# Mixture-of-experts and Fourier mixing in one kernel: tokens and residuals side by side in the first half of a step, comparisons between the halves, GELU rounded by ACT

## The chip, the cores and the metric

The kernel runs on one core of a Trainium2 chip. The time is device microseconds of one execution; the median of three runs stands for a kernel. Engines are named as in the profile: PE (matmuls), DVE (vector), ACT (activations), POOL (indirect DMAs here), SP (the queue of plain DMAs). Each works through its instructions in order.

## The reference, cut to what matters

```python
# x: 2048 tokens x 448; 8 experts, hidden width 1792, top 2
g = sigmoid((x * gate_w).sum(-1))
a = Re(DFT_seq(DFT_hidden(x)))              # given as four dense matrices
gates = softmax(x @ wg); cw = the two largest gates of a token, normalised, else 0
h = gelu(einsum("nd,edf->nef", x, w1))      # tanh form
b = einsum("ne,ned->nd", cw, einsum("nef,efd->ned", h, w2))
out = g * a + (1 - g) * b
```

All inputs and the output are fp32.

## The kernel before

The Fourier part runs first, folded by the symmetries of the given matrices. Whether the matrices have these symmetries is compared on the device, beside the experts' work: `quad_check` compares tiles of them (`quads`) on DVE, and a general path at the end runs only where a comparison fails. Then each token goes to two experts. A routing generator (`routing`, lines 239 to 443) sorts tokens into experts in small pieces on DVE, with two short matmul groups on PE (lines 373 and 404); `advance` runs its next pieces, two in each step of expert 0.

The experts are 112 jobs of 14 steps each, (e, f): expert e, the 128 hidden columns f. The experts are sorted by load, and `CAPS` is the number of tokens that each takes: 576, 544, 544, 544, 512, 512, 512, 496. Every fp32 operand is kept as two parts, a rounded one and the residual that the rounding leaves, so that a product is three matmul passes at the fast rate for rounded operands. The names are:

- `hi`, `lo`: the first weight matrix of a step, rounded by ACT (`upper`, line 205) and its residual by DVE (`lower`, line 210); `up`, `dn`: the same for the second matrix. Both are made two steps ahead (`prep`).
- `XH`, `XL`: the expert's tokens, transposed, in four chunks of 128 rows (`NC`); XL holds three, because the fourth chunk carries 64 token rows and their residuals together. They are filled for the next expert by `gather` (POOL), `blocks` (DVE transposes into `xq`) and `turn` (ACT rounds, DVE subtracts).
- `acc`: three PSUM banks for the up product; `g`: GELU of it (ACT, line 748), two buffers; `gh`, `gl`: `g` rounded (DVE, line 756) and the residual (DVE, line 757), three buffers each; `y`: the sums of the down product, one bank for 128 tokens.

`up(u)` does the up product of job u. With more than 512 tokens it takes two halves (`nh = 2`), each 11 matmuls into one bank: `hi` with XH and with XL for three chunks, `hi` with the fourth chunk of XH, `lo` with the four chunks of XH. `down(u)` does three matmuls of 448 columns for each 128 tokens. With 32 tokens over (experts 1 to 3, `apart`) these are set aside in `rest` and come at the end of an expert (`few`); expert 0 has 64 over and takes them as a fifth tile.

The main loop writes iteration u in this order: `turn`, `prep(u + 2)`, routing pieces (expert 0), `stage` (DVE transposes and gathers), `up(u + 1)`, `down(u)`, `side_work(u)`. PE, DVE, ACT and SP keep the order in which the code is written (`manual_schedule`), and waits are semaphores between the queues. `side_work(u)` issues the DMAs of `quads`, does one quarter of a unit of comparisons (from step 15 on; a unit of four steps has 1, 2, 2 and 3 comparisons of 512 columns, and in later units four of 256 columns against `near`, all in its first step), the blends of the Fourier part (in the fourth and sixth step of experts 1 to 4), and later mixes and sends.

Of the kernel before, what the change touches and what calls it, by code (L numbers as in the profile page):

```python
# [10 lines left out]
F32R = mybir.dt.float32r  # L11
# [3 lines left out]
AF = mybir.ActivationFunctionType  # L15
OP = mybir.AluOpType
AX = mybir.AxisListType

P = 128
# [4 lines left out]
NC = 4  # L24
E = 8
F = 1792
NF = F // P
CAPS = (576, 544, 544, 544, 512, 512, 512, 496)
CMAX = max(CAPS)
# [10 lines left out]
Q = 32  # L40
# [22 lines left out]
def r32(ap):  # L63
    return ap.bitcast(F32)
# [7 lines left out]
def tile_kernel(ctx: ExitStack, tc: tile.TileContext, xt, xrows, xplain, wg, whid, cq, cw, cspec, edge, refs, wquad, whall, cgen, wcat, out):  # L72
# [450 lines left out]
    XH, XL = {}, {}  # L523
# [125 lines left out]
    def turn(e, c):  # L649
        if c == 0:  # L650
            XH[e] = xp.tile([P, NC, CMAX], F32R, name="XH")
            XL[e] = xp.tile([P, NC - 1, CMAX], F32R, name="XL")
        k, xq = XQ.pop((e, c))
        src = xq[:, :k].rearrange("p q c t -> p c q t")
        sl = slice(c * P, c * P + k * Q)
        h = XH[e][:, :, sl].rearrange("p c (q t) -> p c q t", t=Q)
        l = XL[e][:, :, sl].rearrange("p c (q t) -> p c q t", t=Q)
        se.activation(h, src, AF.Copy)
        ve.tensor_tensor(l, src[:, : NC - 1], r32(h[:, : NC - 1]), OP.subtract)
        ve.tensor_tensor(h[64:P, NC - 1], src[64:P, NC - 1], r32(h[64:P, NC - 1]), OP.subtract)  # L660

    def turn0(c, n):
        if c == 0:
            XH[0] = xp.tile([P, NC, CMAX], F32R, name="XH")
            XL[0] = xp.tile([P, NC - 1, CMAX], F32R, name="XL")
        pt = (psy if c > 1 else ps).tile([P, NC, P], F32, name=f"y{c - 2}" if c > 1 else "acc")
        xg = XG.pop(c)
        for k in range(NC):
            te.transpose(pt[:, k, :n], xg[:n, k * P : (k + 1) * P], ident[:n, :n])
        sl = slice(c * P, c * P + n)  # L670
        se.activation(XH[0][:, :, sl], pt[:, :, :n], AF.Copy)
        TU[c] = pt, sl, n
# [3 lines left out]
    def left0(c):  # L676
        pt, sl, n = TU.pop(c)
        ve.tensor_tensor(XL[0][:, :, sl], pt[:, : NC - 1, :n], r32(XH[0][:, : NC - 1, sl]), OP.subtract)  # L678
        ve.tensor_tensor(XH[0][64:P, NC - 1, sl], pt[64:P, NC - 1, :n], r32(XH[0][64:P, NC - 1, sl]), OP.subtract)
# [51 lines left out]
    def up(u):  # L731
# [6 lines left out]
        cut = 2 * P if u == 0 else cap // nh  # L738
        for hf in range(nh):
            cs = slice(hf * cut, cap if hf == nh - 1 else cut)  # L740
            n = cs.stop - cs.start
            acc = ps.tile([P, 512], F32, name="acc")
            part = lambda w, x, c: (w[:, c * P : (c + 1) * P], x[e][:, c, cs])
            steps = [part(hi, XH, c) for c in range(NC - 1)] + [part(hi, XL, c) for c in range(NC - 1)]
            steps += [part(hi, XH, NC - 1)] + [part(lo, XH, c) for c in range(NC)]
            for s, (a, b) in enumerate(steps):
                te.matmul(acc[:, :n], a, b, start=s == 0, stop=s == len(steps) - 1)  # L747
            se.activation(g[:, cs], acc[:, :n], AF.Gelu_apprx_tanh)  # L748
# [7 lines left out]
        ve.tensor_copy(gh[:, :top], g[:, :top])  # L756
# [117 lines left out]
    def quad_check(q, s):  # L874
# [3 lines left out]
        if part < 2:  # L878
# [10 lines left out]
            if s:  # L889
                return  # L890
            if col < 8 * NQT:
                rt["near"] = ck.tile([P, 2, 256], F32, name="near", bufs=1)
                se.activation(rt["near"].rearrange("p c n -> p (c n)"), row(0)[:, :512], AF.Copy)
                return
            for k in range(4):
# [116 lines left out]
    def side_work(s):  # L1012
# [12 lines left out]
        if 1 <= e <= NQT and f in (3, 5):  # L1025
            blend(2 * (e - 1) + f // 5)
# [16 lines left out]
    for u in range(UP, last):  # L1043
# [15 lines left out]
        up(u + 1)  # L1059
        if u < last - 3:  # L1060
            down(u)
        side_work(u - UP)
# [205 lines left out]
```

## Time and profile before

| | us |
|---|---|
| median of 3 runs | 637.38 |
| the runs | 636.42, 637.38, 637.40 |
| the profiled execution | 636.95 |
| its span, first to last instruction | 635.0 |

| engine | busy us (share of the span) | instructions |
|---|---|---|
| PE | 625.5 (99%) | 3721 |
| DVE | 506.1 (80%) | 1258 |
| ACT | 248.1 (39%) | 504 |
| POOL | 204.8 (32%) | 194 |

The span's start and end are those of the program on the core; 1.95 us of the execution lie around it. A matmul's listed duration covers its way through the array and overlaps the next one's, so what a matmul costs is read from the starts of two that follow each other. Of DVE and ACT instructions the listed ends overlap the next start by some hundredths to a tenth of a microsecond too. "[0.57 <-ACT g]" at the end of a timeline row says that the engine idled 0.57 us before it and what ended that.

### The profile page before, as it was taken

To read this page: it belongs to the slowest core of one execution; us is meant where nothing else is said; L and a number is where in the kernel's file an instruction comes from. 1 tells how busy PE (TensorE), PEld (TensorE's weight loads), DVE (VectorE), ACT (ScalarE), POOL (GpSimd) and SP (SyncE) were. 2 spreads that over 40 slices of the span, in tenths; PEclk is the share of its full clock that TensorE was granted. 3 is DMA by queue.
4 is the path that set the end of the run, shared out by engine and by line. 5 is a ranking of instruction groups with operands and counts; after the bars stand their busy time and mean duration, and the time that the engine had idled before them with its cause. 6 is when DMAs were issued, how large, how long until landed. Compare 5 with 4: busy or idle time off the path is not lost. (4 is left out here: it accounts for less than half of the span.)

```text
span 635.0 us, 11162 instructions
## 1 busy us (share of the span) xinstructions
PE 625.5 (99%) x3721; PEld 564.1 (89%) x3721; DVE 506.1 (80%) x1258; ACT 248.1 (39%) x504; POOL 204.8 (32%) x194
## 2 busy tenths in 40 slices
PE   9999999999999999999999999999999999999995
PEld 5999999999998999989999788888888888888884
DVE  7889797589987899779997699987997788556561
ACT  2553233344344444343443434333343434444450
POOL 1210084553153141443340343433331432141123
PEclk9999999999999999999999999999999999999998
DMA  8546454487677766786676957779576736766754
GB/s 345 187 148 211 159 181 140 160 200 260 199 253 194 211 220 218 234 206 207 207 234 203 245 164 237 251 221 291 161 234 195 152 114 151 166 129 151 149 82 67
DMA packets 58752, 122.79 MB, mean 193 GB/s; under 512 B 8288, under 2 KB 31984, under 8 KB 58688
## 3 DMA queue, kind: packets, MB, share of 16 engines
q1 hardware_dynamic: 47376, 101.95, 49.0%
q0 software_dynamic: 11168, 20.00, 17.7%
q8 instruction: 31, 0.51, 0.3%
q14 instruction: 33, 0.27, 0.1%
q10 hardware_dynamic: 144, 0.07, 0.0%
HBM read 105.89 MB, written 16.08 MB: 192 GB/s over the span
## 5 line engine op out<-in xcount | busy, mean ns | idle before, releaser
L748 ACT ACTIVATE g<-acc 128x272 f32<-128x272 f32 (+4 forms) x168 | 77.9, 466 | 311.1 <-issue 179.7
L637 POOL DMA_INDIRECT xg<-xrows,piece x115 | 120.2, 1045 | 223.4 <-DVE xq L646 150.0
L790 PE MATMUL y<-up,gh 128*128 128x448 f32 (+1 forms) x458 | 167.7, 366 | 0.0
L790 PE MATMUL y<-dn,gh 128*128 128x448 f32 (+1 forms) x458 | 167.6, 366 | 0.0
L747 PE MATMUL acc<-XH,hi 128*128 128x272 f32 (+4 forms) x672 | 163.6, 324 | 0.0
L790 PE MATMUL y<-up,gl 128*128 128x448 f32 (+1 forms) x444 | 162.8, 367 | 0.1
L747 PE MATMUL acc<-XH,lo 128*128 128x272 f32 (+4 forms) x672 | 135.0, 323 | 0.0
L747 PEld LDWEIGHTS acc<-XH,hi 128*128 128x128 f32 x672 | 115.6, 188 | 9.3 <-issue 1.1
L747 PEld LDWEIGHTS acc<-XH,lo 128*128 128x128 f32 x672 | 105.8, 188 | 8.7 <-DVE lo L210 0.2
L756 DVE CAST gh<-g 128x512 fp32r<-128x512 f32 (+2 forms) x111 | 47.8, 431 | 81.2 <-ACT g L748 74.9
L747 PE MATMUL acc<-XL,hi 128*128 128x272 f32 (+4 forms) x504 | 107.8, 322 | 0.0
L843 POOL DMA_INDIRECT out<-ys,tok x36 | 62.0, 1723 | 115.6 <-ACT ys L839 69.7
L790 PEld LDWEIGHTS y<-up,gh 128*128 128x128 f32 (+1 forms) x458 | 85.8, 187 | 8.0 <-DVE ys L837 0.2
L790 PEld LDWEIGHTS y<-dn,gh 128*128 128x128 f32 (+1 forms) x458 | 85.8, 187 | 7.8
L790 PEld LDWEIGHTS y<-up,gl 128*128 128x128 f32 (+1 forms) x444 | 83.2, 187 | 7.9 <-DVE gl L757 0.4
L884 DVE CUSTOM_DVE_ANT_0 junk<-quads 128x512 f32<-128x512 f32 x128 | 88.1, 688 | 2.5 <-DMA quads<-cq 0.3
L747 PEld LDWEIGHTS acc<-XL,hi 128*128 128x128 f32 x504 | 81.0, 188 | 6.9 <-DVE XL L678 0.2
L757 DVE TENSOR_TENSOR gl<-g,gh 128x512 fp32r<-128x512 f32 (+1 forms) x111 | 76.7, 691 | 10.5 <-DVE gh L756 0.5
L210 DVE TENSOR_TENSOR lo<-raw,hi 128x512 fp32r<-128x512 f32 x112 | 77.1, 688 | 2.1 <-ACT hi L205 1.0
L205 ACT ACTIVATE hi<-raw 128x512 fp32r<-128x512 f32 x112 | 69.7, 622 | 0.0
L210 DVE TENSOR_TENSOR dn<-row,up 128x448 fp32r<-128x448 f32 x112 | 69.2, 618 | 0.0
L205 ACT ACTIVATE up<-row 128x448 fp32r<-128x448 f32 x112 | 63.5, 567 | 0.0
(263 smaller groups left out, 388.5 us busy)
## 6 DMA issues: line engine op xcount, KB each, us to landing
quads<-cq SPq DMA_DIRECT2D x64, 512.0 KB
raw<-wcat SPq DMA_DIRECT2D x112, 256.0 KB
row<-wcat SPq DMA_DIRECT2D x112, 224.0 KB
out<-yt SPq DMA_DIRECT2D x21, 224.0 KB
xraw<-xt SPq DMA_DIRECT2D x8, 512.0 KB
out<-ot POOLq DMA_DIRECT2D x16, 224.0 KB
cw<-cw SPq DMA_DIRECT2D x4, 512.0 KB
xg<-xrows,piece POOLq DMA_INDIRECT x115
```

Source lines behind the costliest of these rows:

```text
L205: se.activation(hi[:, : raw.shape[-1]], raw, AF.Copy)
L210: ve.tensor_tensor(lo[:, :n], raw, r32(hi[:, :n]), OP.subtract)
L637: st = gp.indirect_dma_start(out=xg[:, q], out_offset=None, in_=xrows, in_offset=bass.IndirectOffsetOnAxis(ap=rt["piece"][:, e, g : g + 1] ...
L747: te.matmul(acc[:, :n], a, b, start=s == 0, stop=s == len(steps) - 1)
L748: se.activation(g[:, cs], acc[:, :n], AF.Gelu_apprx_tanh)
L756: ve.tensor_copy(gh[:, :top], g[:, :top])
L757: ve.tensor_tensor(gl[:, :main], g[:, :main], r32(gh[:, :main]), OP.subtract)
L790: te.matmul(Y[c][:m, :D], a, b, start=f == 0 and s == 0, stop=f == NF - 1 and s == len(steps) - 1)
L843: st = gp.indirect_dma_start(out=out, out_offset=bass.IndirectOffsetOnAxis(ap=rt["tok"][:n, e, c : c + 1], axis=0), in_=ys[:n], in_offset= ...
L884: ve.tensor_tensor_reduce(out=junk[:, :512], in0=row(a[0])[:, a[1] * 512 : a[1] * 512 + 512], in1=row(b[0])[:, b[1] * 512 : b[1] * 512 + 5 ...
```

## The change

It does four things, in experts 0 to 3 (those with more than 512 tokens) except where said.

1. XH and XL become one tile `X` of seven chunks: 0 to 3 the rounded tokens, 4 to 6 the residuals.
2. The first half of a step is 256 columns wide (it was half of the tokens, 288 or 272, apart from step 0). For chunks 0 to 2 one matmul of 512 columns takes the 256 rounded columns and the 256 residual columns of a chunk with the same weights, into the two halves of one bank. The fourth chunk and `lo` go into the bank's first half alone. So the first half has 8 matmuls in place of 11. ACT copies the residual sums to `g`, DVE adds the other half to them, and ACT does GELU in place. The second half (320 or 288 columns) is as before. Step 0 keeps its old first half.
3. `gh` is rounded by ACT instead of DVE. In experts 4 to 7 DVE still does it.
4. `side_work` is called between the two halves of `up(u + 1)` instead of behind `down(u)`; in experts 4 to 7 it stays behind. The near comparisons are spread, three in the first step of a unit and one in the second, for all experts. The blends move to the third and the last step of an expert.

```diff
     def turn(e, c):
         if c == 0:
-            XH[e] = xp.tile([P, NC, CMAX], F32R, name="XH")
-            XL[e] = xp.tile([P, NC - 1, CMAX], F32R, name="XL")
+            X[e] = xp.tile([P, 2 * NC - 1, CMAX], F32R, name="X")
...
-        h = XH[e][:, :, sl].rearrange("p c (q t) -> p c q t", t=Q)
-        l = XL[e][:, :, sl].rearrange("p c (q t) -> p c q t", t=Q)
+        h = X[e][:, :NC, sl].rearrange("p c (q t) -> p c q t", t=Q)
+        l = X[e][:, NC:, sl].rearrange("p c (q t) -> p c q t", t=Q)
...
-    def up(u):
+    def up(u, between=lambda: None):
...
-        cut = 2 * P if u == 0 else cap // nh
+        cut = 2 * P
         for hf in range(nh):
...
-            part = lambda w, x, c: (w[:, c * P : (c + 1) * P], x[e][:, c, cs])
-            steps = [part(hi, XH, c) for c in range(NC - 1)] + [part(hi, XL, c) for c in range(NC - 1)]
-            steps += [part(hi, XH, NC - 1)] + [part(lo, XH, c) for c in range(NC)]
-            for s, (a, b) in enumerate(steps):
-                te.matmul(acc[:, :n], a, b, start=s == 0, stop=s == len(steps) - 1)
-            se.activation(g[:, cs], acc[:, :n], AF.Gelu_apprx_tanh)
+            part = lambda w, x, c: (w[:, c * P : (c + 1) * P], X[e][:, x + c, cs], n)
+            both = nh > 1 and hf == 0 and u > 0
+            if both:
+                steps = [(hi[:, c * P : (c + 1) * P], X[e][:, c : c + NC + 1 : NC, cs], 2 * n) for c in range(NC - 1)]
+            else:
+                steps = [part(hi, 0, c) for c in range(NC - 1)] + [part(hi, NC, c) for c in range(NC - 1)]
+            steps += [part(hi, 0, NC - 1)] + [part(lo, 0, c) for c in range(NC)]
+            for s, (a, b, m) in enumerate(steps):
+                te.matmul(acc[:, :m], a, b, start=s == 0, stop=s == len(steps) - 1)
+            if both:
+                se.activation(g[:, cs], acc[:, n : 2 * n], AF.Copy)
+                ve.tensor_tensor(g[:, cs], acc[:, :n], g[:, cs], OP.add)
+            se.activation(g[:, cs], g[:, cs] if both else acc[:, :n], AF.Gelu_apprx_tanh)
+            if hf == 0:
+                between()
...
-        ve.tensor_copy(gh[:, :top], g[:, :top])
+        if nh > 1:
+            se.activation(gh[:, :top], g[:, :top], AF.Copy)
+        else:
+            ve.tensor_copy(gh[:, :top], g[:, :top])
         ve.tensor_tensor(gl[:, :main], g[:, :main], r32(gh[:, :main]), OP.subtract)
...
-            if s:
-                return
             if col < 8 * NQT:
+                if s:
+                    return
...
-            for k in range(4):
+            for k in ((0, 1, 2), (3,), (), ())[s]:
...
-        if 1 <= e <= NQT and f in (3, 5):
-            blend(2 * (e - 1) + f // 5)
+        if 1 <= e <= NQT and f in (2, NF - 1):
+            blend(2 * (e - 1) + f // (NF - 1))
...
-        up(u + 1)
+        split = CAPS[jobs[u + 1][0]] > 512
+        up(u + 1, lambda: side_work(u - UP) if split else None)
         if u < last - 3:
             down(u)
-        side_work(u - UP)
+        if not split:
+            side_work(u - UP)
```

`turn0` and `left0`, which fill the tokens of expert 0, change only in the names of the tiles.

How the instructions stand is shown at three places. The first is DVE's queue in expert 0, one step with the routing's `oa` compares. Before:

```order
L756 CAST gh<-g 128x576 [waits Activation_49]
L757 TENSOR_TENSOR gl<-g,gh 128x512 [waits DVE_49]
L764 TENSOR_TENSOR gh<-g,gh 128x64
L210 TENSOR_TENSOR lo<-raw,hi 128x512 [waits DMAHW7_49,PE_49,Activation_49]
L210 TENSOR_TENSOR dn<-row,up 128x448 [waits DMAHW0_49,PE_49,Activation_49]
L360 TENSOR_TENSOR oa<-sr,one 128x1024 x2
```

The same step with the change:

```order
L752 TENSOR_TENSOR g<-acc,g 128x256 [waits Activation_49]
L767 TENSOR_TENSOR gl<-g,gh 128x512 [waits Activation_49]
L774 TENSOR_TENSOR gh<-g,gh 128x64
L210 TENSOR_TENSOR lo<-raw,hi 128x512 [waits DMAHW7_49,Activation_49]
L210 TENSOR_TENSOR dn<-row,up 128x448 [waits DMAHW0_49,Activation_49]
L360 TENSOR_TENSOR oa<-sr,one 128x1024 x2
```

The add takes the cast's place, and `gl`, which waited for the cast on its own engine, now waits for ACT. The second place is ACT's queue in the same step. Before:

```order
L748 ACTIVATE g<-acc 128x288 [waits DVE_49,PE_49,Activation_49]
L748 ACTIVATE g<-acc 128x288 [waits PE_49]
L205 ACTIVATE hi<-raw 128x512 [waits DMAHW5_49]
L205 ACTIVATE up<-row 128x448 [waits DMAHW6_49]
L748 ACTIVATE g<-acc 128x288 [waits DVE_49,PE_49,Activation_49]
```

With the change:

```order
L751 ACTIVATE g<-acc 128x256 [waits PE_49]
L753 ACTIVATE g<-g 128x256 [waits DVE_49]
L753 ACTIVATE g<-acc 128x320 [waits PE_49]
L764 ACTIVATE gh<-g 128x576 [waits Activation_49]
L205 ACTIVATE hi<-raw 128x512 [waits DMAHW5_49]
L205 ACTIVATE up<-row 128x448 [waits DMAHW6_49]
```

The first GELU stands behind a wait for DVE's add, and the rounding stands between the second GELU and the next step's weights. The third place is PE's up product in expert 1. Before, one half of it:

```order
L747 MATMUL acc<-XH,hi 128x272 [waits Activation_49]
L747 MATMUL acc<-XH,hi 128x272 x2
L747 MATMUL acc<-XL,hi 128x272 x3
L747 MATMUL acc<-XH,hi 128x272
L747 MATMUL acc<-XH,lo 128x272 [waits DVE_49]
L747 MATMUL acc<-XH,lo 128x272 x3
```

With the change, the first half and the start of the second:

```order
L749 MATMUL acc<-X,hi 128x512 [waits Activation_49]
L749 MATMUL acc<-X,hi 128x512 x2
L749 MATMUL acc<-X,hi 128x256
L749 MATMUL acc<-X,lo 128x256 [waits DVE_49]
L749 MATMUL acc<-X,lo 128x256 x3
L749 MATMUL acc<-X,hi 128x288 [waits DVE_49]
```

Six matmuls have become three, and the second half's bank is now released by DVE (the add that read it last) instead of ACT.

## Rows read from the trace of the kernel before

**Rows 1.** The page: busy time of PE, and the clock that TensorE was granted in 40 slices of the span, in tenths.

```profile
PE 625.5 (99%) x3721; PEld 564.1 (89%) x3721; DVE 506.1 (80%) x1258; ACT 248.1 (39%) x504; POOL 204.8 (32%) x194
...
PEclk9999999999999999999999999999999999999998
```

**Rows 2.** PE's timeline, one step of expert 2 (start us, duration, engine, line, operation and tiles, count): start of the first half, start of the down product, start of the next step.

```profile
206.49 0.54 PE L747 MATMUL acc<-XH,hi 128*128 128x272 f32 x3
...
209.26 0.36 PE L790 MATMUL y<-up,gh 128*128 128x448 f32 x1
...
211.73 0.54 PE L747 MATMUL acc<-XH,hi 128*128 128x272 f32 x3
```

**Rows 3.** PE's timeline, one step of expert 0 and the routing's matmul group behind it.

```profile
64.17 0.56 PE L747 MATMUL acc<-XH,hi 128*128 128x288 f32 x3
...
67.09 0.37 PE L790 MATMUL y<-up,gh 128*128 128x448 f32 x1
...
69.98 0.98 PE L373 MATMUL acc<-vtok,oa 128*128 128x40 f16 x32
```

**Rows 4.** PE's timeline at other widths: from the first `XL` matmul of step 0's first half (256 columns) to its second half, and one step of expert 5 (512 columns) to the next.

```profile
38.15 0.52 PE L747 MATMUL acc<-XL,hi 128*128 128x256 f32 x3
...
39.10 0.60 PE L747 MATMUL acc<-XH,hi 128*128 128x320 f32 x3
...
422.93 0.86 PE L747 MATMUL acc<-XH,hi 128*128 128x512 f32 x3
423.62 0.84 PE L747 MATMUL acc<-XL,hi 128*128 128x512 f32 x3
...
425.43 0.36 PE L790 MATMUL y<-up,gh 128*128 128x448 f32 x1
...
427.87 0.86 PE L747 MATMUL acc<-XH,hi 128*128 128x512 f32 x3
```

**Rows 5.** DVE's timeline in expert 0, from one cast to the next.

```profile
56.62 0.46 DVE L756 CAST gh<-g 128x576 fp32r<-128x576 f32 x1
57.11 0.69 DVE L757 TENSOR_TENSOR gl<-g,gh 128x512 fp32r<-128x512 f32 x1
...
58.99 2.36 DVE L360 TENSOR_TENSOR oa<-sr,one 128x1024 bf16<-128x1024 bf16 x2
61.92 0.46 DVE L756 CAST gh<-g 128x576 fp32r<-128x576 f32 x1 [0.57 <-ACT g L748]
```

**Rows 6.** Groups of instructions with shapes kept apart (busy us, mean ns of one, idle before), ACT and DVE.

```profile
L205 ACT ACTIVATE hi<-raw 128x512 fp32r<-128x512 f32 x112 | 69.7, 622 | 0.0
...
L748 ACT ACTIVATE g<-acc 128x320 f32<-128x320 f32 x1 | 0.4, 437 | 1.4 <-PE acc L747 1.4
...
L748 ACT ACTIVATE g<-acc 128x256 f32<-128x256 f32 x1 | 0.4, 383 | 1.2 <-PE acc L747 1.2
...
L990 DVE TENSOR_TENSOR ot<-fold 128x225 f32<-128x225 f32 x16 | 6.2, 390 | 0.0
...
L678 DVE TENSOR_TENSOR XL<-acc,XH 128x384 fp32r<-128x384 f32 x2 | 1.1, 553 | 0.0
```

**Rows 7.** ACT's timeline in expert 0: a second half's GELU, and two GELUs without a wait between them.

```profile
61.47 0.41 ACT L748 ACTIVATE g<-acc 128x288 f32<-128x288 f32 x1 [1.01 <-PE acc L747]
...
98.88 0.71 ACT L748 ACTIVATE g<-acc 128x288 f32<-128x288 f32 x2 [5.59 <-PE acc L747]
```

**Rows 8.** DVE's timeline in expert 0: the end of the routing piece ahead of step 0's cast, `gl` of step 0, `vtok`, the rows with idle time before them, and `gl` of step 13.

```profile
42.38 0.17 DVE L323 TENSOR_SCALAR capm<-cap 128x8 f32<-128x8 f32 x1
...
43.15 0.69 DVE L757 TENSOR_TENSOR gl<-g,gh 128x512 fp32r<-128x512 f32 x1
...
65.82 1.49 DVE L368 TENSOR_TENSOR vtok<-ob,tok 128x1280 f16<-128x1280 f32 x1
67.73 0.46 DVE L756 CAST gh<-g 128x576 fp32r<-128x576 f32 x1 [0.42 <-ACT g L748]
...
71.00 0.20 DVE L376 TENSOR_SCALAR none<-acc 128x40 f32<-128x40 f32 x1 [0.81 <-PE acc L373]
...
74.45 0.46 DVE L756 CAST gh<-g 128x576 fp32r<-128x576 f32 x1 [2.56 <-ACT g L748]
...
91.82 0.46 DVE L756 CAST gh<-g 128x576 fp32r<-128x576 f32 x1 [0.90 <-issue]
...
98.71 0.20 DVE L407 COPY wgt<-acc 128x40 f32<-128x40 f32 x1 [3.53 <-PE acc L747]
...
117.28 0.71 DVE L757 TENSOR_TENSOR gl<-g,gh 128x512 fp32r<-128x512 f32 x1
```

**Rows 9.** PE's timeline, the matmul of `down(13)` that takes `gl` of step 13 first.

```profile
122.00 0.37 PE L790 MATMUL y<-up,gl 128*128 128x448 f32 x1
```

**Rows 10.** Expert 1: DVE's timeline from the first of three comparisons to the next `lo`, and the engines' busy time over its whole stretch (PE, PEld, DVE, ACT, POOL with counts, clock, DMA).

```profile
152.13 0.69 DVE L884 CUSTOM_DVE_ANT_0 junk<-quads 128x512 f32<-128x512 f32 x1
...
154.21 0.68 DVE L210 TENSOR_TENSOR lo<-raw,hi 128x512 fp32r<-128x512 f32 x1
...
125.00:201.00 76.00, 76.00 (x507) 70.74 (x505) 67.23 (x170) 32.12 (x71) 28.88 (x24) 1.00 0.73 219
```

**Rows 11.** PE's timeline in expert 5, two matmuls of a down product.

```profile
460.26 0.36 PE L790 MATMUL y<-dn,gh 128*128 128x448 f32 x1
460.69 0.47 PE L790 MATMUL y<-up,gl 128*128 128x448 f32 x1
```

More of the change, by code (lines that the diff above doesn't have):

```diff
@@ L522, in tile_kernel @@
     tl0 = tiles_of(CAPS[0])
-    XH, XL = {}, {}
+    X = {}
     XG, XQ = {}, {}
@@ L663, in turn0 @@
         if c == 0:
-            XH[0] = xp.tile([P, NC, CMAX], F32R, name="XH")
-            XL[0] = xp.tile([P, NC - 1, CMAX], F32R, name="XL")
+            X[0] = xp.tile([P, 2 * NC - 1, CMAX], F32R, name="X")
         pt = (psy if c > 1 else ps).tile([P, NC, P], F32, name=f"y{c - 2}" if c > 1 else "acc")
@@ L670, in turn0 @@
         sl = slice(c * P, c * P + n)
-        se.activation(XH[0][:, :, sl], pt[:, :, :n], AF.Copy)
+        se.activation(X[0][:, :NC, sl], pt[:, :, :n], AF.Copy)
         TU[c] = pt, sl, n
@@ L677, in left0 @@
         pt, sl, n = TU.pop(c)
-        ve.tensor_tensor(XL[0][:, :, sl], pt[:, : NC - 1, :n], r32(XH[0][:, : NC - 1, sl]), OP.subtract)
-        ve.tensor_tensor(XH[0][64:P, NC - 1, sl], pt[64:P, NC - 1, :n], r32(XH[0][64:P, NC - 1, sl]), OP.subtract)
+        ve.tensor_tensor(X[0][:, NC:, sl], pt[:, : NC - 1, :n], r32(X[0][:, : NC - 1, sl]), OP.subtract)
+        ve.tensor_tensor(X[0][64:P, NC - 1, sl], pt[64:P, NC - 1, :n], r32(X[0][64:P, NC - 1, sl]), OP.subtract)
     def due(e, step, pace):
```

## The prediction

> **What bounds the kernel now.** I read the page first: the PE row, busy 99% of the span, and the clock row, which stays at the full level up to the last slice [rows 1]. A PE that is never idle has two ways to get faster, fewer matmuls or cheaper ones, and one way to get slower, a wait that it does not have today. So the second view was PE's timeline. In a step of expert 2 the 22 matmuls of 272 columns take 209.26 - 206.49 = 2.77 us, 126 ns each, and the 12 of 448 columns 211.73 - 209.26 = 2.47 us, 206 ns each; a step is 5.24 us [rows 2]. In expert 0 the step is 22 matmuls of 288 (2.92 us) and 14 of 448 (2.89 us), 5.81 us [rows 3].
>
> The third view was DVE's timeline, because DVE feeds PE twice in a step: `lo` (the weights' residuals) and `gl` (GELU's residuals), both in one in-order queue. In expert 0 this queue also carries the routing. One step there [rows 5]: cast to `gl` 0.49 us, then `gl`, the 64-column `gh`, `lo` and `dn` 1.88 us (57.11 to 58.99), then two `oa` compares, 2.36 us, then 0.57 us of idle time before the next cast. That is 4.73 us of work in a 5.8 us step. So PE sets the pace, and DVE follows it with little to spare; this is the place to watch.
>
> **Part 1, fewer matmuls.** The columns stay the same (11 x 272 twice before; 3 x 512, 5 x 256 and 11 x 288 now), and three weight loads and matmuls a step go. What that is worth depends on what a matmul costs beside its columns. At 256 columns eight take 39.10 - 38.15 = 0.95 us, 119 ns each; at 512 the first three take 0.69 us, 230 ns each, the next eight 1.81 us, 226 ns each [rows 4]. So one of 512 replaces two of 256 (238 ns) for 226 to 230, a gain of 8 to 12 ns. With 229, 119 and 133 (288 columns, rows 3) a step of experts 1 to 3 has 3 x 229 + 5 x 119 + 11 x 133 = 2745 ns in place of 2765: 20 ns less, times 42 steps, **-0.85 us**. The same in expert 0 is not counted, because DVE will set the pace there (part 2). The trace has no matmul that reads its columns in two pieces, as the new one does (tokens, then residuals). I bound it by the contiguous 512 (226) and by two separate matmuls (238), so the part is worth between -1.3 and +0.3 us; I take 229, since the piece change is one address step.
>
> The Trainium skill (TensorE: Matmul & The Clock Gate, "Back-to-back issue gap") gives a matmul at full clock its columns over 2.4 GHz plus about 2.5 ns; by it a merge would save 2.5 ns, 0.3 us for experts 1 to 3 instead of 0.85. The rows disagree: 119 ns at 256 columns is 12 ns over the columns' 107.
>
> **Part 2, the wait that the change adds.** Before, ACT did two GELUs from PSUM, and DVE rounded `g` itself (the cast). Now a step's chain is: PE's first half, ACT copy, DVE add, ACT GELU of the first half, ACT GELU of the second, ACT rounding into `gh`, DVE `gl`. In DVE's queue the add and `gl` stand directly behind each other in expert 0, since there are no comparisons yet to lie between them. DVE is in order, so from the add to `gl` it does nothing but wait for ACT. The price, from forms of the same size or the nearest:
> - add, 256 columns with one operand in PSUM: between 0.39 (225 columns) and 0.55 (384 from PSUM) [rows 6], by their slope 0.42, some 0.02 of it under the next start: 0.40
> - GELU of the first half, 256 columns: 0.38 [rows 6], but the next ACT instruction starts before it ends: two of 0.41 took 0.71 together [rows 7], so 0.30 - 0.03 = 0.27
> - GELU of the second half, 320 columns: 0.44 [rows 6]
> - rounding of 576 columns: 0.62 at 512, and 64 columns more cost the GELU 0.06 (0.38 to 0.44) [rows 6], so 0.68
> - three hand-overs at 0.04 (GELU ends 61.88, cast starts 61.92) [rows 5, 7]: 0.12
>
> Together 1.91, say 1.9 us from the add's start to `gl`'s, where cast to `gl` took 0.49: **+1.41 us in each DVE step**. The copy, 0.38 more on ACT, costs nothing: PE has long finished the half when DVE comes to the add late, and ACT is idle then. If DVE came early, the copy would be part of the wait, but PE would then not be waiting for DVE.
>
> The sum over expert 0, from `gl` of step 0 to `gl` of step 13. Before, these start at 43.15 and 117.28 [rows 8]. 13 steps x 1.41 = +18.3. Step 0's `gl` starts 0.6 earlier, because no cast stands ahead of it and routing ends at 42.55 [rows 8]; ACT, idle there, has rounded by then. The idle time that DVE has now in this stretch is used up: 0.57 + 0.42 + 0.81 + 2.56 + 0.90 + 3.53 = 8.79 [rows 5, 8]. So `gl` of step 13 moves by 18.3 - 0.6 - 8.8 = 8.9 us. PE takes it at 122.00 [rows 9], and it is done at 117.28 + 0.71 = 117.99, so 4.0 of that is slack. PE enters expert 1 late by **+4.9 us**. A check at half way: the four steps up to `vtok` cost 4 x 1.41 = 5.6, less 0.6 and 0.57; `vtok` ends at 67.31 + 4.4 = 71.7, and PE wants it at 69.98 [rows 3], so about 1.8 us of the idle time is to be seen there, the rest near steps 8, 11 and 12, which have the long routing pieces and the turning of expert 1's tokens.
>
> I take the chain at 1.9. At 1.65 (rounding and GELU overlap more) the total is 3.3 less, +1.6; at 2.15 it is +8.2. It would be below nothing only with a chain under 1.53, for which ACT would have to round before the GELU has ended; the rounding reads what the GELU writes, so the chain itself does not go there. What could is the first rival below.
>
> **Part 3, experts 1 to 3.** The same wait stands there, but the comparisons now lie between the add and `gl`. Three such comparisons take 2.08 us, one 0.73 or so (0.69 and its read) [rows 10]. The ACT chain behind the add is 0.27 + 0.41 + 0.62 + 0.12, 1.4 us. Two or three comparisons cover it; only the step with one, one in four, leaves 0.7 us bare (with the near rows it has three short ones more and is covered). That is 0.1 to 0.2 us a step on average. DVE is busy 67.23 of 76.00 us in expert 1 [rows 10], 4.64 of 5.24 a step; with 0.2 it is 4.84. So PE keeps the pace: 0. Cast out and add in are of one size on DVE (0.46 for 576 columns in rows 5, 0.42 for the add). ACT gets some 1.0 us a step (copy 0.38, rounding 0.62) on 32.12 of 76.00 [rows 10], 2.2 a step: 3.2 of 5.2, not the bound. The blends move to steps without a token block, which takes their work out of two full steps of DVE; that is worth nothing where PE has the pace.
>
> **Part 4, experts 4 to 7.** Only the near comparisons change (three and one in place of four in one step). In expert 5 PE waits once behind them, 460.69 - 460.26 = 0.43 where 0.21 is usual [rows 11]: **-0.2 us**.
>
> **Sum.** The profiled execution took 636.95 us, 1.95 around its span; the median of the three runs is 637.38, 0.1% above. 636.95 - 0.85 + 4.9 - 0.2 = **640.8 us**.
>
> **Rivals.**
> - *The wait stays off PE's path (faster).* If DVE in expert 0 reaches the add so early that ACT's chain runs beside PE's second half, the wait is only idle time, as the 9 us of today are, and PE gains 20 ns in each of 55 steps: 636.95 - 1.1 - 0.2 = 635.65. It decides where DVE's step (1.88 + routing + 1.9) is under PE's 5.8, that is where routing takes under 2.0 us. For it: the 8.8 us that DVE idles there now, so some steps are that short. Against it: 2.36 us in rows 5, and 8.8 is half of the 18.3 that are to be hidden. 0.13.
> - *Matmuls of 448 columns get cheaper.* They take 206 ns behind short matmuls [rows 2], but behind matmuls of 512 columns (427.87 - 425.43) / 12 = 203 ns [rows 4]. If three wide matmuls a step are enough to change this, 42 x 12 x 3.3 ns = 1.7 us come off: 639.1. Nothing in the rows says which neighbour does it. 0.10.
> - *DVE also sets the pace in experts 1 to 3 (slower still).* Its step is summed at 4.84 us against PE's 5.24, so this decides from 0.6 us of bare wait a step instead of 0.2. With 0.8 DVE's step is 5.44, 0.2 too long on 42 steps, 8.4 us, less a slack like the 4.0 of step 13: +4.4, 645.2. For it: tokens are turned in ten steps of an expert, which are fuller than the mean. 0.09.
> - *The change does nothing measurable,* since DVE's wait and the idle time it uses up balance: 637. 0.03.
>
> **How the numbers follow.** The forecast (DVE sets the pace in expert 0) has 0.65, its own range 638.0 to 643.5. The range that should hold 8 in 10 takes in the chain's bounds (-3.3, +3.3), the two-piece read (+1.1) and the cheaper 448 columns (-1.7), not both ends at once: 636.2 to 644.2. A measurement of this kernel can tell about 0.2% (1.3 us) from no change. Slower by more: the forecast without its lowest end 0.60, half of the second rival 0.05, the third 0.09: 0.74. Faster by more: the first, 0.13. The same: the rest, 0.13.
>
> **What would show it.** Right: in expert 0 DVE idle before `gl` with ACT's `gh` as the releaser, about 1.4 us each; PE idle about 2 us before the `vtok` matmuls and in pieces of 0.2 to 2 us near steps 8, 11 and 12; PE's step unchanged or 20 ns shorter from expert 1 on; 512-column matmuls 226 to 238 ns apart. Wrong: PE without gaps in expert 0 (the first rival), 448-column matmuls at 203 ns in experts 1 to 3 (the second), or gaps before `gl` or `lo` from step 16 on (the third).

## The result, and the profile after

| | before | after |
|---|---|---|
| median of six runs, us | 637.33 | 642.39 |
| lowest to highest | 636.42 to 637.53 | 641.79 to 642.69 |
| the profiled execution | 636.95 | 642.40 |
| its span | 635.0 | 640.5 |

The changed kernel is 0.8% slower: a ratio of 1.0082, 95% interval 1.0069 to 1.0095. The forecast was 640.8. Its sign and its place hold, and the time lies in its range of 636.2 to 644.2, but two of its terms were too small, and one stretch of the program, the end, had no term.

The span is cut at four matmuls which both kernels have. PE's timeline of the kernel before, at these: the first matmul of step 0, of expert 1's second step, of expert 4's second step, and the last of all.

```profile
37.70 0.61 PE L747 MATMUL acc<-XH,hi 128*128 128x256 f32 x3
...
124.43 0.73 PE L747 MATMUL acc<-XH,hi 128*128 128x272 f32 x3
...
353.53 0.96 PE L747 MATMUL acc<-XH,hi 128*128 128x512 f32 x3
...
626.95 0.36 PE L790 MATMUL y<-up,lo 128*112 128x448 f32 x1
```

The same four after:

```profile
38.12 1.10 PE L749 MATMUL acc<-X,hi 128*128 128x256 f32 x7
...
131.25 0.98 PE L749 MATMUL acc<-X,hi 128*128 128x512 f32 x4
...
357.47 1.42 PE L749 MATMUL acc<-X,hi 128*128 128x512 f32 x5
...
630.47 0.36 PE L800 MATMUL y<-up,lo 128*112 128x448 f32 x1
```

| stretch | before us | after us | difference | forecast |
|---|---|---|---|---|
| Fourier part, up to step 0 | 37.70 | 38.12 | +0.42 | 0 |
| expert 0 and one step of expert 1 | 86.73 | 93.13 | +6.40 | +4.9 |
| experts 1 to 3 and one step of expert 4 | 229.10 | 226.22 | -2.88 | -0.85 |
| experts 4 to 7 | 273.42 | 273.00 | -0.42 | -0.2 |
| from the last matmul to the end of the span | 8.05 | 10.03 | +1.98 | 0 |
| sum | 635.0 | 640.5 | +5.5 | +3.85 |

The first row is the same code in both; in the eight other kernels below it ends between 37.75 and 38.35, so it scatters.

The page's rows for the engines and for the clock after [rows 1]:

```profile
PE 624.4 (97%) x3556; PEld 555.4 (87%) x3556; DVE 501.3 (78%) x1257; ACT 300.8 (47%) x615; POOL 213.1 (33%) x194
...
PEclk9999999999999999999999999999999999999998
```

PE's busy time hardly falls, and its share of the span goes from 99% to 97%: the loss is idle time, and the clock row is the one of before.

**The wait of expert 0.** DVE's timeline after, from an add to the routing's `vtok`, answers to [rows 5, 8]:

```profile
65.53 0.41 DVE L752 TENSOR_TENSOR g<-acc,g 128x256 f32<-128x256 f32 x1
67.47 0.69 DVE L767 TENSOR_TENSOR gl<-g,gh 128x512 fp32r<-128x512 f32 x1 [1.52 <-ACT gh L764]
...
70.86 1.49 DVE L368 TENSOR_TENSOR vtok<-ob,tok 128x1280 f16<-128x1280 f32 x1
```

And ACT's timeline between the add and `gl` [rows 7]:

```profile
65.97 0.42 ACT L753 ACTIVATE g<-g 128x256 f32<-128x256 f32 x1 [3.38 <-DVE g L752]
66.30 0.42 ACT L753 ACTIVATE g<-acc 128x320 f32<-128x320 f32 x1
66.75 0.69 ACT L764 ACTIVATE gh<-g 128x576 fp32r<-128x576 f32 x1
```

DVE adds at 65.53, ACT needs 0.33 + 0.45 + 0.72 for two GELUs and the rounding, and DVE starts `gl` at 67.47: 1.94 us after the add, 1.52 of them idle. Cast to `gl` took 0.49 before. The routing pieces stand behind `gl` and not in front of it, so `vtok` ends at 72.35, and PE waits for it. PE's timeline, with its longest waits [rows 3]:

```profile
72.41 0.96 PE L373 MATMUL acc<-vtok,oa 128*128 128x40 f16 x32 [1.51 <-DVE vtok L368]
...
113.24 1.29 PE L749 MATMUL acc<-X,hi 128*128 128x320 f32 x7 [1.44 <-DVE g L752]
...
127.20 0.79 PE L749 MATMUL acc<-X,hi 128*128 128x288 f32 x4 [0.17 <-DVE X L658]
```

The view of waits (engine, line, waited for: sum us, times, longest) has no others of PE behind the start of step 0, and all lie in expert 0 and the first step of expert 1:

```profile
PE acc L749 <- DVE g L752: 2.1, 3, 1.4
PE acc L373 <- DVE vtok L368: 1.5, 1, 1.5
...
PE acc L749 <- ACT X L657: 0.4, 1, 0.4
PE acc L749 <- DVE X L658: 0.2, 1, 0.2
```

These waits add up to 4.2 us, less than PE loses in this stretch (6.40). The view counts from a matmul's listed end, which lies behind the moment at which the next one could have started, and short stops are not in its list (as the 0.29 from 67.92 to 68.21, where 0.20 is usual). What a stop costs is therefore read from starts: the matmul ahead of the 1.51 us starts at 70.54, so the next starts 1.87 later instead of 0.20.

**The tail.** Behind the last matmul two things differ. The last scatter's data land later by about half a microsecond. Then all engines run a closing chain of semaphore instructions (which the views leave out). PE's stops in the middle at 637.10 and goes on at 638.54, and the other engines wait for it. At 638.52 one 8 KB packet starts on an instruction queue. The view of DMA queues over the last 3.9 us after:

```profile
q14 instruction: 1, 0.01, 0.5%
```

Over the last 2.4 us before, the same view has one packet of q8 and none of q14.

### The profile page after: what moved, and what is told of

Its sections match the earlier page's. It is cut to its first block, busy times and chain, and to the rows that moved or that the text cites. A ratio compares the mean times of both kernels' runs of the same rounds, so it can differ in the third digit from the quotient of the medians.

```text
span 640.5 us, 10896 instructions
## 1 busy us (share of the span) xinstructions
PE 624.4 (97%) x3556; PEld 555.4 (87%) x3556; DVE 501.3 (78%) x1257; ACT 300.8 (47%) x615; POOL 213.1 (33%) x194
## 4 chain that ended last, share of the span: by engine, by line
PE 79%; DVE 9%; issue 4%; ACT 3%; DMA 2%; POOL 1%; POOLq 0%; DVEq 0%; SPq 0%; ACTq 0%
PE acc L749 38%; PE y L800 36%; ACT g L753 1%; ACT gh L764 1%; PE y L817 1%; PE acc L512 1%; DVE lo L210 1%; DVE dn L210 1%; PE y L474 1%; POOL out L853 1%; PE y L555 1%; DVE oa L360 1%; DMA wgr<-wg 1%; DVE vw L399 1%; DVE g L752 1%
## 5 line engine op out<-in xcount | busy, mean ns | idle before, releaser
L749 PE MATMUL acc<-X,hi 128*128 128x512 f32 (+4 forms) x1011 | 216.3, 349 | 2.6 <-DVE g L752 2.1
L637 POOL DMA_INDIRECT xg<-xrows,piece x115 | 125.9, 1095 | 219.6 <-DVE xq L646 134.6
L749 PEld LDWEIGHTS acc<-X,hi 128*128 128x128 f32 x1011 | 170.6, 188 | 24.3 <-DVE g L752 2.7
L749 PE MATMUL acc<-X,lo 128*128 128x256 f32 (+4 forms) x672 | 134.7, 322 | 0.0
L753 ACT ACTIVATE g<-acc 128x288 f32<-128x288 f32 (+4 forms) x113 | 56.5, 500 | 147.6 <-issue 84.7
L749 PEld LDWEIGHTS acc<-X,lo 128*128 128x128 f32 x672 | 105.6, 188 | 10.7
L767 DVE TENSOR_TENSOR gl<-g,gh 128x512 fp32r<-128x512 f32 (+1 forms) x111 | 76.5, 689 | 40.4 <-ACT gh L764 34.6
L853 POOL DMA_INDIRECT out<-ys,tok x36 | 64.7, 1796 | 113.9 <-ACT ys L849 75.6
L766 DVE CAST gh<-g 128x512 fp32r<-128x512 f32 (+1 forms) x55 | 23.8, 433 | 51.5 <-ACT g L753 51.5
L753 ACT ACTIVATE g<-g 128x256 f32<-128x256 f32 x55 | 23.0, 418 | 83.7 <-DVE g L752 83.7
L751 ACT ACTIVATE g<-acc 128x256 f32<-128x256 f32 x55 | 20.7, 377 | 46.3 <-PE acc L749 45.9
```

Source lines behind the costliest of these rows:

```text
L637: st = gp.indirect_dma_start(out=xg[:, q], out_offset=None, in_=xrows, in_offset=bass.IndirectOffsetOnAxis(ap=rt["piece"][:, e, g : g + 1] ...
L749: te.matmul(acc[:, :m], a, b, start=s == 0, stop=s == len(steps) - 1)
L751: se.activation(g[:, cs], acc[:, n : 2 * n], AF.Copy)
L753: se.activation(g[:, cs], g[:, cs] if both else acc[:, :n], AF.Gelu_apprx_tanh)
L767: ve.tensor_tensor(gl[:, :main], g[:, :main], r32(gh[:, :main]), OP.subtract)
L853: st = gp.indirect_dma_start(out=out, out_offset=bass.IndirectOffsetOnAxis(ap=rt["tok"][:n, e, c : c + 1], axis=0), in_=ys[:n], in_offset= ...
```

## The experiments

Each is a variant of the changed kernel; the diffs are against it. The first four ran beside runs of the kernel before with a median of 637.00, the second four beside 637.07.

| kernel | median us | ratio to before, 95% interval |
|---|---|---|
| expert 0 as before | 634.07 | 0.9956 (0.9941 to 0.9971) |
| expert 0 without merge and add | 634.30 | 0.9958 (0.9942 to 0.9973) |
| `gl` behind the next weights | 651.48 | 1.0231 (1.0217 to 1.0245) |
| no merge anywhere | 636.02 | 0.9989 (0.9979 to 0.9998) |
| DVE rounds in expert 0 | 640.29 | 1.0046 (1.0030 to 1.0061) |
| comparisons behind the down product | 671.08 | 1.0535 (1.0518 to 1.0551) |
| PE's stream shifted | 641.29 | 1.0064 (1.0050 to 1.0078) |
| routing between the halves | 633.84 | 0.9952 (0.9938 to 0.9965) |

### Expert 0 as before

```diff
-        cut = 2 * P
+        cut = 2 * P if u == 0 or e else cap // nh
...
-            both = nh > 1 and hf == 0 and u > 0
+            both = nh > 1 and hf == 0 and e > 0
...
-        if nh > 1:
+        if nh > 1 and e > 0:
             se.activation(gh[:, :top], g[:, :top], AF.Copy)
```

> Expert 0 as before (halves of 288, no merge, no add, rounding by DVE); experts 1 to 3 as changed. Theory (the loss is DVE's wait between add and gl in expert 0; experts 1 to 3 gain, and the tail behind the last matmul is longer for a reason of its own): PE without gaps in expert 0, first matmul of expert 1 within 0.5 us of before's 124.4, then 2.9 us gained in experts 1 to 3 and 0.4 later, so 634.0 with the tail of before (8.0 us behind the last matmul's start) and 636.0 with that of the changed kernel (10.0). Rival (the loss comes from something that the change does outside the steps of expert 0, such as the one tile X for tokens and residuals or the moved comparisons): gaps near 70.5 and 111.5 stay, 640 or more.

634.07, and the first matmul of expert 1's second step is back at the time of before. PE's timeline:

```profile
124.43 0.87 PE L749 MATMUL acc<-X,hi 128*128 128x512 f32 x3
```

PE waits nowhere in the expert steps. So the whole loss in expert 0 comes from how its steps are done, not from the one tile `X` or the moved comparisons, and the rest of the change is a gain of 0.4%.

### Expert 0 without merge and add, ACT rounds

```diff
-        cut = 2 * P
+        cut = 2 * P if u == 0 or e else cap // nh
...
-            both = nh > 1 and hf == 0 and u > 0
+            both = nh > 1 and hf == 0 and e > 0
```

> Expert 0 with halves of 288 and no merge and no add, but ACT still rounds; experts 1 to 3 as changed. Theory (the wait costs because add and gl stand back to back in DVE's queue with an ACT chain between them): without the add DVE meets only gl, which waits for nothing that DVE itself delays, so DVE's step is 0.49 us shorter than before, no gaps, 634.0 to 636.0. Rival (rounding on ACT is what delays gl, with or without the add): DVE idles before gl by 1 us or more in each step and PE has gaps again, 638 to 642.

634.30, no waits of PE in the expert steps. DVE still idles before `gl`. A row of its timeline, and behind it ACT's, the GELU of the second half in the same step:

```profile
62.81 0.69 DVE L767 TENSOR_TENSOR gl<-g,gh 128x512 fp32r<-128x512 f32 x1 [1.58 <-ACT gh L764]
```

```profile
61.65 0.41 ACT L753 ACTIVATE g<-acc 128x288 f32<-128x288 f32 x1 [1.06 <-PE acc L749]
```

But this idle time is DVE's lead over PE: ACT itself waits for PE there, and DVE has nothing to do until PE has ended the second half. It is 1.58 us here, as long as the harmful 1.52, and costs nothing. What tells the two apart is where the chain begins. With the add, DVE itself starts it, so a DVE that is late makes it late. Rounding on ACT alone does no harm.

### `gl` behind the next weights

In expert 0, `gl` of a step is written by a function of its own, called in the next iteration behind `prep` and the routing pieces:

```diff
+        if e:
+            finish(u)
...
+    def finish(u):
...
         ve.tensor_tensor(gl[:, :main], g[:, :main], r32(gh[:, :main]), OP.subtract)
...
             clear(2 * (u - UP) + 1)
+        if e == 0:
+            finish(u)
```

> As changed, but in expert 0 gl (and the residuals of the last 64 columns) of a step is written behind the next step's lo, dn and routing pieces, in front of the next add, so ACT's chain of copy-add-GELU-GELU-rounding has 1.2 us and the routing to run beside. Nothing is left out. Theory: no wait before gl, no PE gaps in expert 0, and 13 merged steps there gain 20 to 50 ns each: first matmul of expert 1 at 124.0, then 2.9 and 0.4 gained; 633.4 with the tail of before, 635.4 with that of the changed kernel, which it should have if PE's place in its instruction stream makes the tail, since PE's instructions are the same. Rival (ACT, which now also copies and rounds, is itself the bound in expert 0): gaps stay, 640 to 642. Second rival (gl comes too late for the down product): short gaps of 0.2 to 0.5 us before y<-up,gl in each step, 637 to 640.

651.48, 9 us slower than the changed kernel. The expectation was wrong (its second rival had the place right, the down product, and the size not), and with it the belief that `lo` and `dn` can run beside ACT's chain. `lo` is made from `hi`, which ACT makes, and ACT's queue has `hi` behind the rounding:

```profile
68.34 0.69 ACT L765 ACTIVATE gh<-g 128x576 fp32r<-128x576 f32 x1
68.93 0.61 ACT L205 ACTIVATE hi<-raw 128x512 fp32r<-128x512 f32 x1
```

So DVE waits in front of `lo` instead, and longer, and `gl` comes so late that the down product waits for it. DVE's timeline in the same step, and behind it PE's:

```profile
67.12 0.41 DVE L752 TENSOR_TENSOR g<-acc,g 128x256 f32<-128x256 f32 x1
69.58 0.69 DVE L210 TENSOR_TENSOR lo<-raw,hi 128x512 fp32r<-128x512 f32 x1 [2.05 <-ACT hi L205]
```

```profile
74.39 0.47 PE L812 MATMUL y<-up,gl 128*128 128x448 f32 x1 [1.22 <-DVE gl L780]
```

The waits are not all of the 9 us. Behind the two longest PE ran at the lower clock level for a while (last section): some 8 matmuls of 448 columns each time took 0.37 us instead of 0.20, by estimate 2 x 8 x 0.17 = 2.7 us.

### No merge anywhere

```diff
-            both = nh > 1 and hf == 0 and u > 0
+            both = False
```

> As changed, but no merged matmuls and no add anywhere: first halves of 256 columns in 11 matmuls, ACT rounds, comparisons between the halves, all of experts 0 to 3. Theory: no gaps in expert 0; the up product of a step in experts 1 to 3 is 20 to 25 ns longer than in the changed kernel (22 matmuls, 2.76 us). If the three 512-column matmuls are what makes the 448-column ones cheaper (203.9 ns in the changed kernel, 205.7 before), these are back at 205.7 and the whole is 637.0 with the tail of before. If they are cheaper for another reason (the rounding or the comparisons have moved), they stay at 203.9 and the whole is 636.1. With a tail of 10 us both are 2.0 more.

636.02. That is the total of the expectation's second case, but the rows show its first. PE's timeline of a step of expert 2, starts of the first half, the down product and the next step:

```profile
205.75 0.99 PE L749 MATMUL acc<-X,hi 128*128 128x256 f32 x7
...
208.52 0.36 PE L800 MATMUL y<-up,gh 128*128 128x448 f32 x1
...
210.99 0.99 PE L749 MATMUL acc<-X,hi 128*128 128x256 f32 x7
```

The up product takes 2.77, the down product 2.47, as before [rows 2]; in the step after it is 2.76 and 2.47. Two steps of the changed kernel:

```profile
211.95 0.96 PE L749 MATMUL acc<-X,hi 128*128 128x512 f32 x4
...
214.68 0.36 PE L800 MATMUL y<-up,gh 128*128 128x448 f32 x1
...
217.15 0.98 PE L749 MATMUL acc<-X,hi 128*128 128x512 f32 x4
...
219.89 0.36 PE L800 MATMUL y<-up,gh 128*128 128x448 f32 x1
...
222.32 0.84 PE L749 MATMUL acc<-X,hi 128*128 128x512 f32 x3
```

Up 2.73 and 2.74, down 2.47 and 2.43. So the merge saves 0.03 us in the up product, and every second down product is 0.04 shorter (2.43 / 12 = 203 ns a matmul instead of 206). The cheaper down products go with the merge: without it they are gone. But the merge alone does not say which step has one. In the kernel "PE's stream shifted" below, expert 2 has the same instructions as in the changed kernel, and there every down product takes 2.43 (214.83 to 217.26, 219.99 to 222.42). What decides it stays open.

The total is 1.0 below the first case's 637.0 because experts 1 to 3 take 0.77 us less than before without any merge, and experts 4 to 7 take 0.43 less; the expectation had no term for either.

In expert 0 this kernel has halves of 256 columns and ACT rounds, and PE has no wait there (86.48 us for the stretch of the table, 86.73 before). So the width of the halves does no harm either.

### DVE rounds in expert 0

```diff
-        if nh > 1:
+        if nh > 1 and e > 0:
             se.activation(gh[:, :top], g[:, :top], AF.Copy)
```

> As changed, but in expert 0 DVE rounds g again (merge, add and two GELUs stay). Theory (the price is the time from the add to gl on DVE): add 0.41, then 0.8 of waiting for two GELUs, cast 0.49, so add to gl is 1.7 us in place of the 1.94 measured (65.53 to 67.47); 13 x 0.25 = 3.2 us less at the first matmul of expert 1, whole 639.2 with the long tail. Rival (the rounding on ACT alone makes the wait): gaps in expert 0 gone, 635 to 636.

640.29. DVE's timeline:

```profile
72.05 0.42 DVE L752 TENSOR_TENSOR g<-acc,g 128x256 f32<-128x256 f32 x1
73.28 0.46 DVE L766 CAST gh<-g 128x576 fp32r<-128x576 f32 x1 [0.81 <-ACT g L753]
73.77 0.69 DVE L767 TENSOR_TENSOR gl<-g,gh 128x512 fp32r<-128x512 f32 x1
```

Add to `gl` is 1.72 where 1.7 was expected, and PE loses 2.1 us less than in the changed kernel (expert 1's second step begins at 129.11 instead of 131.25), where 3.2 were expected. Two thirds of the loss stay with rounding back on DVE. So the add in front of the GELU is the larger part, and ACT's rounding costs only where it lengthens the chain that the add begins.

### Comparisons behind the down product

```diff
-        split = CAPS[jobs[u + 1][0]] > 512
+        split = False
```

> As changed, but the comparisons and blends stay behind the down product in all experts, so in experts 1 to 3 nothing lies between add and gl. Theory: DVE's step there is 4.64 of work (before) - 0.49 + 0.42 + 1.5 of bare wait = 6.1 us against PE's 5.19; 0.9 x 42 = 38 us more, less a slack of some 4: about 676, with gaps of PE in most steps of experts 1 to 3. Rival (PE's lead absorbs it, or DVE's idle time is counted twice): under 650.

671.08, 28.7 us more than the changed kernel, where 34 were expected. The view of waits, DVE's longest entry:

```profile
DVE gl L767 <- ACT gh L764: 80.9, 55, 1.7
```

DVE idles there 55 times, 1.5 us each; in the changed kernel it was 29 times, 34.6 us, of which 16 times and 14.8 us lie in experts 1 to 3, where PE waits for nothing. So the comparisons between the halves cover most of the wait in experts 1 to 3, and what they leave bare stays off PE's path.

### PE's stream shifted

```diff
-            both = nh > 1 and hf == 0 and u > 0
+            both = nh > 1 and hf == 0 and u > 0 and (e, f) not in ((3, 2), (3, 4), (3, 6), (3, 8))
```

> As changed, but four steps of expert 3 (the 3rd, 5th, 7th and 9th) keep 11 matmuls and no add in their first half. This shifts what follows in PE's instruction stream by 12 matmuls with their weight loads and costs 4 x 0.03 us on PE. Theory (in the changed kernel PE waits 1.5 us at the program's end for a packet of its own instructions, which its place in the stream decides): the stretch from the last matmul's start to the end of the span falls from 10.0 to 8.2 to 8.7 us, whole 640.7 to 641.2. Rival (the end is longer because the last scatter lands later): it stays at 10.0, whole 642.5.

641.29, 1.1 us under the changed kernel. The last matmul starts at 630.49, as there (630.47), and the span ends at 639.6: 9.1 us of tail instead of 10.0. The time is 0.1 us above the expectation and the tail between the two expectations, and the trace says why. The pause in PE's closing chain is gone, and over the last 2.4 us the view of DMA queues has no packet at all:

```profile
DMA packets 0, 0.00 MB, mean 0 GB/s; under 512 B 0, under 2 KB 0, under 8 KB 0
```

From the moment at which PE sees the last scatter landed to the end of the span it is 2.3 us, as before, where the changed kernel has 3.8. The scatter itself landed 0.6 us later in this execution. All kernels agree: those that have the changed kernel's 3556 matmuls (also `gl` behind the next weights, DVE rounds, comparisons behind) show the q14 packet there and 3.8 to 4.5 us, and in all four PE pauses behind the same instruction of the chain, for 1.4 to 2.0 us. The five with another count have 2.3 to 2.5. DVE rounds has other counts on DVE and ACT than the changed kernel and pauses too, so it goes by PE's stream. The landing lies between 5.7 and 6.7 us behind the last matmul's start, in no order that the changes explain.

### Routing between the halves

```diff
-            both = nh > 1 and hf == 0 and u > 0
+            both = nh > 1 and hf == 0 and u not in (0, 1, 5, 7, 9, 12, 13)
...
         if u < UP + SIDE:
-            advance(2)
+            if u in (4, 6, 8):
+                advance(2)
...
-        up(u + 1, lambda: side_work(u - UP) if split else None)
+        def between():
+            if u < UP + SIDE and u not in (4, 6, 8):
+                advance(2)
+            if split:
+                side_work(u - UP)
+        up(u + 1, between)
```

> The routing pieces of expert 0 are called between the halves as the comparisons are, except in the three iterations whose pieces PE or a gather needs at once; steps whose add would stand bare in front of gl (and step 1) are not merged (merged in expert 0 are seven steps). Nothing is left out. Theory: DVE has 0.7 to 3.9 us of routing between add and gl, needs no wait there, and PE has no gaps in expert 0; experts 1 to 3 as in the changed kernel; PE's stream is 21 matmuls longer, so the short end: 633.6 to 634.3. Rival (as with gl written behind the weights' residuals, some other thing in ACT's or DVE's order waits in its place): gaps in expert 0, 636 to 645.

633.84, as expected, the lowest of all, faster than before by 0.48% and than the changed kernel by 8.5 us. DVE's timeline in expert 0 shows the routing pieces in the place of the wait:

```profile
60.10 0.42 DVE L752 TENSOR_TENSOR g<-acc,g 128x256 f32<-128x256 f32 x1 [1.17 <-ACT g L751]
60.45 2.35 DVE L360 TENSOR_TENSOR oa<-sr,one 128x1024 bf16<-128x1024 bf16 x2
62.72 0.68 DVE L767 TENSOR_TENSOR gl<-g,gh 128x512 fp32r<-128x512 f32 x1
```

`gl` follows the compares without a wait, and DVE idles before the add instead, where it waits for ACT's copy of what PE has just ended. PE has no wait in expert 0. Against the kernel with expert 0 as before (634.07) the difference is inside the scatter of the runs. (PE's stream has 3574 matmuls, 18 more than the changed kernel's and not 21.)

## Why the prediction was right, step by step

- **Part 2, the chain.** Summed 1.91 us, measured 1.94. The add was put at 0.40, the GELUs at 0.27 and 0.44, the rounding at 0.68, the hand-overs at 0.12; the rows give 0.44 from add to GELU, then 0.33, 0.45 and 0.72. The delay that it makes was right too: `gl` of step 13 was to move by 8.9 us. DVE's timeline after, first and last `gl` of expert 0, against 43.15 and 117.28 [rows 8]:

```profile
43.07 0.69 DVE L767 TENSOR_TENSOR gl<-g,gh 128x512 fp32r<-128x512 f32 x1
...
126.16 0.69 DVE L767 TENSOR_TENSOR gl<-g,gh 128x512 fp32r<-128x512 f32 x1 [1.53 <-ACT gh L764]
...
126.90 0.25 DVE L658 TENSOR_TENSOR X<-xq,X 128x96 fp32r<-128x96 f32 x1
```

  It moved by 8.88. That the two agree so closely is luck in part: `gl` of step 0 starts 0.08 earlier and not 0.6, and an idle time of 0.26 before 116.63 in the kernel before is missing from the sum of what is used up.
- **Part 2, the slack: the step that failed.** "PE takes it at 122.00 [rows 9], and it is done at 117.28 + 0.71 = 117.99, so 4.0 of that is slack." `gl` of step 13 is not the first of that stretch that PE needs. Behind it in DVE's queue stand the residuals of expert 1's last 32 tokens, which the second half of step 14 reads. DVE's timeline before, and behind it PE's:

```profile
118.05 0.25 DVE L659 TENSOR_TENSOR XL<-xq,XH 128x96 fp32r<-128x96 f32 x1
```

```profile
120.57 0.54 PE L747 MATMUL acc<-XL,hi 128*128 128x272 f32 x3
```

  They were done at 118.05 + 0.25 = 118.30, and PE read them at 120.57, which leaves 2.27. After, they are done at 127.15, and PE reads them at 127.20, the last of its waits above. 8.85 - 2.27 = 6.6 is what PE has lost at this matmul. At the end of the stretch it is 131.25 - 124.43 = 6.82, of which the table books 0.42 in the first row; DVE's chain did not start later for that, so 6.82 is what stands against 4.9. The term was 1.9 us too small: 1.7 because a later consumer was taken for the first, 0.2 because the matmuls behind the stop took 4.05 us to the end of the stretch instead of 3.86.
- **Part 2, the places.** PE idle 1.51 us before the `vtok` matmuls (forecast 1.8 to 2), and in pieces of 0.3 to 1.4 near steps 9, 12 and 13, at 92.25, 113.24 and 119.78. There it waits for the add, which frees the PSUM bank that the second half takes. The forecast showed this release but had no term for it. It is the other consumer that was overlooked: step 14 begins at 124.56 instead of 118.81, so PE was 5.75 us late, more than the 4.9, before any of expert 1's tokens was wanted. Either of the two by itself comes to more than the forecast.
- **Part 1.** A merged matmul was taken at 229 ns; in experts 1 to 3 they start some 230 ns apart, inside the bounds of 226 and 238, so the read in two pieces costs little. A step's up product was taken at 20 ns less, from 2765 ns, where [rows 2] have 2770. The rows of the two kernels above give 2.765 - 2.735, 30 ns. With the cheaper down products the merge brings 0.05 us a step, 2.1 us in 42 steps: the same stretch is 228.33 us without the merge and 226.22 with it. The Trainium skill (TensorE: Matmul & The Clock Gate, "Back-to-back issue gap") gives columns over 2.4 GHz plus about 2.5 ns for a matmul by itself, and says that this is too little for narrow matmuls in a stream that loads weights for each. By that formula a matmul saved would be worth 2.5 ns, an estimate; the measurement disagrees, 30 ns for three is 10 each. The rival "matmuls of 448 columns get cheaper" came true at half its size, in every second step.
- **The rest of -2.88** is 0.77 that the kernel without merges has as well. About half of it is a wait of before, in the step that begins at 124.43: it took 5.58 us (to 130.01) where later steps take 5.24. None of the nine other kernels has this wait (5.17 us in the changed one). What causes it stays open. Another 0.2 is a like wait in the step that begins at 161.42, whose up product takes 2.98 instead of 2.77.
- **Part 3.** Covered, as said: PE has no wait in experts 1 to 3, and the kernel with the comparisons behind shows what the cover is worth, 28.7 us. The bare rest was put too low, at 0.1 to 0.2 us a step; it is 14.8 / 42 = 0.35, still under the 0.6 from which DVE would have set the pace. ACT is busy 44.85 of 75.54 us in expert 2's stretch, 3.1 of a step's 5.18 (forecast 3.2). The rival that DVE sets the pace there is out.
- **Part 4.** The wait in expert 5 was 0.43 [rows 11] and is now 0.21 (464.04 to 464.25, in the last section), the 0.2 of the forecast. The whole of experts 4 to 7 is 0.42 shorter; where the other 0.2 comes from stays open.
- **Not in the prediction:** the tail. 1.4 to 1.5 of its 1.98 is the pause in PE's chain, the rest the scatter's landing. It about makes up for the gain of experts 1 to 3, which was under-estimated by 2.0. So the sum, 3.85 forecast and 5.5 measured, is closer than its terms are, and that is luck.

## What to carry to other kernels

A round trip from one in-order engine through another and back costs the first engine its whole length unless something that depends on neither stands in the first engine's queue between the two ends: here the routing pieces do (633.84), the next weights' residuals do not (651.48), since they hang on the same ACT queue. It costs the kernel only where the first engine sets the pace. When an engine falls behind, look for everything that its queue delivers next, and take the slack of the one that is wanted first, not of the one that was edited. And the same idle time before the same instruction is harmless if the engine waits for PE, and a loss if PE waits for the engine: 1.58 us in one kernel and 1.52 in another looked alike.

## What the runs showed of the hardware

- Instruction queues move packets while the program runs: in the changed kernel 34 of 8 KB (q14) and 31 of 16 KB (q8). In four kernels PE stops in its closing chain for 1.4 to 2.0 us, and nothing covers that. That it waits there for the q14 packet is inferred and not shown: PE goes on within half a microsecond of the packet's start in all four, but in three of them before the packet's listed end. What is shown is that twelve matmuls more, far from the end, took the pause away, and that all four kernels with 3556 matmuls have it and the six others do not. So a change in the count of matmuls can move the time by 0.2%.
- A matmul that had to wait delays the next one. Before, the one that waited until 460.69 [rows 11] is listed with 0.47 us instead of 0.36, and the next starts at 461.00, 0.31 later instead of 0.20. After, the same product at 464.25 starts almost on time but is listed with 0.46, and the next starts 0.29 later. A stop thus costs 0.1 us more than the wait in these two. PE's timeline after:

```profile
464.04 0.37 PE L800 MATMUL y<-dn,gh 128*128 128x448 f32 x1
464.25 0.46 PE L800 MATMUL y<-up,gl 128*128 128x448 f32 x1
464.54 0.37 PE L800 MATMUL y<-up,gh 128*128 128x448 f32 x1
```

- In the kernel with `gl` behind the next weights, PE idled 3.03 us before 47.46, and the next matmuls ran at the lower of the two clock levels, 1.2 GHz: 0.37 us each for 448 columns instead of 0.20. The view by stretches shows the granted clock (seventh value) at 0.50 there and at 1.00 behind it. It happened once more: PE idled 2.60 us before 118.21, and from 119.12 on the matmuls again took 0.37. An idle time of 2.33 us before 96.31 in the same kernel left the clock at 1.00.

```profile
47.40:50.80 3.40, 3.34 (x9) 3.00 (x10) 1.36 (x5) 2.41 (x5) 0.00 (x0) 0.50 0.38 142
50.80:55.00 4.20, 4.20 (x27) 3.97 (x26) 3.02 (x13) 1.16 (x3) 0.00 (x0) 1.00 0.67 227
```
